# Six of twenty weight loads issued as 120 and 8 rows

## The chip, the core and the metric

The kernel runs on one core of a Trainium2 chip. The metric is the device time of one execution in microseconds (us); less is better. A core has a matrix engine (PE, whose weight loads the profile lists apart as PEld), three engines for elementwise work (DVE, ACT, POOL), a sequencer that here issues every data transfer (SP), and 16 DMA engines that move the bytes.

## What is computed

Block-sparse attention (4 batches, 8 heads, 768 positions, head size 64, blocks of 32), followed by a gated channel mixer over the 512 channels. Cut to what matters:

```python
mask = |blk_i - blk_j| <= 1, or either block is the first or the last, or a sampled block
attn = softmax(where(mask, q @ k.T / sqrt(64), -1e9));  x = attn @ v   # (4, 768, 512)
x_prev = x shifted by one position
xk = mu_k * x + (1 - mu_k) * x_prev;  xr = mu_r * x + (1 - mu_r) * x_prev
k = maximum(xk @ w_k, 0)            # w_k: 512 x 1024
v = (k * k) @ w_v                   # w_v: 1024 x 512
out = sigmoid(xr @ w_r) * v         # w_r: 512 x 512
```

The three weight matrices arrive as 8-byte floats and are turned on the chip into pairs of 4-byte parts.

## The kernel before

**Attention.** The 24 query blocks are worked through in 26 units. Each of the first 22 handles one query block of all four batches and all heads: SP fetches the queries (`q`, L305), the keys (`KA`, L284 and L332) and the values (`VA`, L297 and L349), PE forms scores (`s`, L402), DVE and ACT make the softmax, and PE multiplies by the values (`o`, L436 for the first four units, L475 after). Three of the key blocks and three of the value blocks of a unit are sampled, so SP reads their numbers from `packed` (L266) and computes the address before each transfer. `KA` and `VA` have few slots: the keys of a later unit may be fetched only when PE has read those of an earlier one.

**Weights.** `weight(i, name, src)` (L179) is called twenty times: i = 0 to 3 for the four row blocks of `w_r`, 4 to 11 for the eight blocks of `w_k`, 12 to 19 for the eight row blocks of `w_v`. Each call plans one transfer "w{i} load" (L187) of 128 rows of 4,096 bytes (512 KB) from HBM into the 128 partitions of `raw`, and then six operations on ACT, DVE and POOL that read `raw` and end in the pair of parts `w`: "size" (`wmag`, L201), "tail", "sign", "join", "hi" (L242) and "lo" (L246).

**Mixer.** Twelve tiles of 256 positions: PE computes `r` (L716), `h` (L737) and `v` (L772), which read the weights `w`.

**Order.** Every operation of the kernel stands in one list, and a table of numbers written out by hand (`ORDER`) gives the sequence in which they are emitted. Each engine runs its own in that sequence and waits on semaphores. The twenty weight loads lie in the first 90 us among the fetches of the first units. SP is the only issuer of transfers, and each transfer counts up one of eight semaphores (DMAHW0 to DMAHW7), used in turn; before it is issued SP waits until the transfer that used that semaphore last, eight issues earlier, has landed.

Of the kernel before, what the change touches and what calls it, by code (L numbers as in the profile page):

```python
# [10 lines left out]
I32 = mybir.dt.int32  # L11
# [8 lines left out]
P = 128  # L20
# [75 lines left out]
def block_sparse_attention_channel_mix(  # L96
# [3 lines left out]
    nc = tc.nc  # L100
# [3 lines left out]
    plan = Plan()  # L104
    unit = WIDE_SCALE if wide else 1.0
    PE, ACT, DVE, POOL, SP = "PE", "ACT", "DVE", "POOL", "SP"

    def buf(shape, dtype, tag, bufs, name, pool=sb):
        return Buf(pool, shape, dtype, tag, bufs, name)
# [4 lines left out]
    def choose(name, ways, **more):  # L114

        engine, ns, port, fn = ways[CHOICE.get(name, 0)]
        if "codes" in more:
            more["code"] = more["codes"][CHOICE.get(name, 0)]
        plan.add(name, engine, ns, fn, port=port, ways=[w[:3] for w in ways], **more)
# [59 lines left out]
    def weight(i, name, src):  # L179

        w = buf([P, 2, 512], F32R, f"w{i}", 1, f"w{i}")
        raw = buf([P, 512, 2], I32, f"w{i}", 1, f"raw{i}")
        f = buf([P, 512], F32, "zr", 3, f"wf{i}")
        mag = buf([P, 512], F32, "kk", 3, f"wmag{i}")
        weight_of[name] = w
        words = 2 if wide else 1
        plan.add(f"w{i} load", SP, 480, lambda: nc.sync.dma_start(  # L187
            raw.ap.rearrange("p x b -> p (x b)")[:, 0 : 512 * words], src.bitcast(I32)), writes=[(raw,)], size=262144 * words)

        def high():  # L190
            return raw.ap[:, :, 1] if wide else raw.ap.rearrange("p x b -> p (x b)")[:, 0:512]

        def shorts(which):
            return raw.ap.bitcast(U16)[:, :, which]

        def halves(dtype, which):
            return f.ap.bitcast(dtype).rearrange("p (a b) -> p a b", b=2)[:, :, which]

        def size():
            if wide:  # L200
                nc.scalar.activation(mag.ap, high().bitcast(F32), AF.Copy, scale=2.0**-111)  # L201

        plan.add(f"w{i} size", ACT, 565, size, reads=[(raw,)], writes=[(mag,)])

        def tail():
            if wide:
                nc.vector.tensor_scalar(out=halves(U16, 0), in0=shorts(1), scalar1=13, scalar2=None, op0=ALU.logical_shift_right)

        def tail_pool():
            if wide:  # L210
                nc.gpsimd.tensor_scalar(out=halves(U16, 0), in0=shorts(1), scalar1=2.0**-13, scalar2=2.0**-14 - 0.5, op0=ALU.mult, op1=ALU.add)

        def tail_act():
            if wide:
                nc.scalar.activation(halves(U16, 0), shorts(1), AF.Copy, scale=2.0**-13, bias=2.0**-14 - 0.5)

        choose(f"w{i} tail", [(DVE, 338, 338, tail), (POOL, 900, 0, tail_pool), (ACT, 640, 0, tail_act)], reads=[(raw,)], writes=[(f, 0)])

        def sign():
            if wide:  # L220
                nc.vector.tensor_scalar(out=halves(U16, 1), in0=shorts(3), scalar1=0x8000, scalar2=None, op0=ALU.bitwise_and)

        def sign_act():
            if wide:
                nc.scalar.activation(halves(F16, 1), high().bitcast(F32), AF.Copy, scale=2.0**-60)

        def sign_pool():
            if wide:
                nc.gpsimd.tensor_scalar(out=halves(F16, 1), in0=high().bitcast(F32), scalar1=2.0**-60, scalar2=None, op0=ALU.mult)

        choose(f"w{i} sign", [(DVE, 338, 338, sign), (ACT, 630, 0, sign_act), (POOL, 1650, 0, sign_pool)], reads=[(raw,)], writes=[(f, 1)])

        def join():
            if wide:
                nc.vector.scalar_tensor_tensor(
                    out=f.ap.bitcast(I32), in0=mag.ap.bitcast(I32), scalar=3, in1=f.ap.bitcast(I32),
                    op0=ALU.logical_shift_left, op1=ALU.bitwise_or)
            else:
                nc.vector.tensor_copy(out=f.ap.bitcast(I32), in_=high())

        plan.add(f"w{i} join", DVE, 603, join, reads=[(raw,), (mag,), (f, 0, 1)], writes=[(f,)], port=603)
        choose(f"w{i} hi", [(ACT, 524, 0, lambda: nc.scalar.copy(w.ap[:, 0, :], f.ap)), (POOL, 632, 0, lambda: nc.gpsimd.tensor_copy(w.ap[:, 0, :], f.ap))],  # L242
               reads=[(f,)], writes=[(w, 0)])

        def rest(by):
            by.tensor_tensor(out=w.ap[:, 1, :], in0=f.ap, in1=w.ap[:, 0, :], op=ALU.subtract)  # L246

        choose(f"w{i} lo", [(DVE, 603, 603, lambda: rest(nc.vector)), (POOL, 1262, 0, lambda: rest(nc.gpsimd))], reads=[(f,), (w, 0)], writes=[(w, 1)])

    def weights():  # L250
        jobs = [(("r", c), w_r[c * P : (c + 1) * P, :]) for c in range(CC)]
        jobs += [(("k", c, f), w_k[c * P : (c + 1) * P, f * 512 : (f + 1) * 512]) for f in range(2) for c in range(CC)]
        jobs += [(("v", f), w_v[f * P : (f + 1) * P, :]) for f in range(FC)]
        for i, job in enumerate(jobs):
            weight(i, *job)
# [388 lines left out]
    def split_x(t, which, i0, many, name):  # L644
# [13 lines left out]

        for h in range(CC // MIX):
            f = buf([P, MIX, tw], F32, "mix", 1, f"{name}f{h}")  # L660
            for i in range(MIX):
                c = h * MIX + i
                d = buf([P, tw], F32, "dif", 1, f"{name}d{c}")
# [17 lines left out]
                ], reads=[(d,), (x, *ready), (mk, 2 + which)], writes=[(f, i)])  # L681
            cs = slice(h * MIX, (h + 1) * MIX)

            def rest(by, f=f, cs=cs):
                by.tensor_tensor(out=dst.ap[:, 1, cs], in0=f.ap, in1=dst.ap[:, 0, cs], op=ALU.subtract)

            choose(f"{name} hi {h}", [
                (ACT, 66 + 0.895 * MIX * tw, 0, lambda f=f, cs=cs: nc.scalar.copy(dst.ap[:, 0, cs], f.ap)),
                (POOL, 290 + 0.72 * MIX * tw, 0, lambda f=f, cs=cs: nc.gpsimd.tensor_copy(dst.ap[:, 0, cs], f.ap)),
# [94 lines left out]
    def mixer():  # L784
        xr = xk = None
        for place, t in enumerate(TILES):
# [21 lines left out]
            for i in range(2):  # L808
# [3 lines left out]
             writes=[(mk, 0)], table="exp")  # L812
# [20 lines left out]
X_FROM = 6  # L833
MOVE_FROM = 4

MIX = 2
LAST = 10
TILES = [*range(1, NTILE - 1), 0, NTILE - 1]
# [156 lines left out]
```

## Time and profile before

| | us |
|---|---|
| median of 3 runs | 518.51 |
| lowest, highest | 516.83, 521.39 |
| the profiled execution, its own time | 516.33 |
| span of that execution from the first to the last instruction | 514.6 |
| PE busy in it | 480.9 (93%) |
| PE idle from 40 to 100 us | 7.15 |
| mean busy share of the 16 DMA engines from 40 to 60 us | 0.98 |

In the rows below, times count from the start of the span. "Busy" leaves out sequencer work. A releaser is what ended an engine's wait; "issue" means that the engine waited for nothing that the profile shows. Queue q1 carries the transfers that the program issues, queues q8 and q14 carry instructions.

### The profile page before, as it was taken

Reading aid. Unit: us, or ns where it says so; the run is one execution under the profiler, and the core shown is the slowest. Engines: PE = TensorE matmul, PEld = TensorE weight load, DVE = VectorE, ACT = ScalarE, POOL = GpSimd, SP = SyncE. Lnnn points to the kernel's source line nnn. Section 1 sums busy time; section 2 is a strip of 40 time slices with the busy share of each in tenths; the row PEclk is TensorE's granted clock in tenths of the full one; section 3 lists DMA queues with packets and bytes.
Section 4 is the critical chain, followed back from the end, with each engine's and each line's share of the span. In section 5 each row is a group of like instructions: output and inputs, shape, how many; then the busy total and the mean of one; then the engine's idle time right before and its main releaser. Section 6 shows DMA issues by size and latency. Waiting matters only on the chain.

```text
span 514.6 us, 18098 instructions
## 1 busy us (share of the span) xinstructions
PE 480.9 (93%) x7384; PEld 399.9 (78%) x7384; DVE 320.7 (62%) x608; ACT 306.4 (60%) x701; POOL 207.5 (40%) x253
## 2 busy tenths in 40 slices
PE   4567899999999998999999999999999999999997
PEld 4254577788788787878778878878778879889896
DVE  3667989786786765775675766664765653334231
ACT  2887988867745646546665846655546574455341
POOL 2435546352610723244442432234543525434531
PEclk9689999999999999999999999999999999999999
DMA  7999999798878889888898888999669653100101
GB/s 265 368 343 379 350 337 310 245 279 249 266 214 252 228 217 270 225 258 236 256 264 240 222 258 265 289 275 340 186 158 309 162 137 85 29 22 20 42 22 41
DMA packets 58052, 114.65 MB, mean 223 GB/s; under 512 B 7665, under 2 KB 20721, under 8 KB 55026
## 3 DMA queue, kind: packets, MB, share of 16 engines
q1 hardware_dynamic: 57970, 113.50, 72.3%
q8 instruction: 58, 0.95, 0.7%
q14 instruction: 24, 0.20, 0.1%
HBM read 77.82 MB, written 6.29 MB: 163 GB/s over the span
## 4 chain that ended last, share of the span: by engine, by line
PE 78%; DMA 8%; SPq 4%; ACT 4%; issue 3%; DVE 2%; POOL 1%; POOLq 0%
PE v L772 22%; PE h_2p L737 7%; PE h_0p L737 6%; PE s L402 6%; PE h_1p L737 6%; PE r_1p L716 6%; PE o L475 6%; PE r_0p L716 6%; PE h_3p L737 6%; DMA VA<-vt 3%; DMA KA<-kt 3%; PE sw L496 2%; PE o L538 2%; ACT p L452 1%; SPq L349 1%
## 5 line engine op out<-in xcount | busy, mean ns | idle before, releaser
L772 PE MATMUL v<-w,k 128*128 128x512 f32 (+1 forms) x600 | 138.9, 385 | 0.0
L772 PEld LDWEIGHTS v<-w,k 128*128 128x128 f32 x600 | 107.9, 188 | 26.7 <-issue 4.6
L402 PE MATMUL s<-KA,q 64*32 64x256 f32 x1408 | 47.6, 391 | 15.7 <-DMA raw<-w_k 10.7
L412 DVE TENSOR_REDUCE nm<-s 128x4 f32<-128x1024 f32 x44 | 53.0, 1215 | 14.3 <-PE s L402 14.0
L452 ACT ACTIVATE p<-s,nm 128x256 f32<-128x256 f32 x144 | 60.6, 479 | 0.6
L455 DVE STREAM_TRANSPOSE r<-p 128x1024 f32<-128x1024 f32 x36 | 43.6, 1229 | 10.9 <-ACT p L452 7.1
L402 PEld LDWEIGHTS s<-KA,q 64*32 64x32 f32 x1408 | 26.2, 109 | 30.2 <-POOL w L246 10.7
L475 PEld LDWEIGHTS o<-VA,pt 128*32 128x32 f32 x2304 | 33.9, 109 | 6.6 <-issue 4.4
L716 PE MATMUL r_0p<-w,xr 128*128 128x512 f32 x144 | 36.8, 400 | 1.3 <-issue 1.3
L475 PE MATMUL o<-VA,pt 128*32 128x65 f32 x2304 | 37.3, 221 | 0.8 <-DMA VA<-vt 0.7
L737 PE MATMUL h_2p<-xk,w 128*128 128x256 f32 x288 | 37.8, 284 | 0.2 <-ACT h_0k L752 0.2
L737 PEld LDWEIGHTS h_0p<-xk,w 128*128 128x128 f32 x288 | 35.6, 189 | 3.0 <-issue 1.6
L737 PE MATMUL h_0p<-xk,w 128*128 128x256 f32 x288 | 37.1, 282 | 0.8 <-issue 0.4
L737 PE MATMUL h_3p<-xk,w 128*128 128x256 f32 x288 | 37.4, 285 | 0.0
L737 PEld LDWEIGHTS h_3p<-xk,w 128*128 128x128 f32 x288 | 35.6, 190 | 2.4 <-issue 1.2
L716 PE MATMUL r_1p<-w,xr 128*128 128x512 f32 x144 | 37.2, 398 | 0.0
L737 PEld LDWEIGHTS h_2p<-xk,w 128*128 128x128 f32 x288 | 35.7, 191 | 1.9 <-issue 0.8
L737 PEld LDWEIGHTS h_1p<-xk,w 128*128 128x128 f32 x288 | 35.3, 189 | 2.3 <-DVE rx L576 1.0
L737 PE MATMUL h_1p<-xk,w 128*128 128x256 f32 x288 | 37.0, 283 | 0.0
L666 ACT ACTIVATE xr_0d<-xt,mk 128x128 f32<-128x128 f32 x48 | 19.3, 403 | 21.9 <-DVE xr_0f L673 15.9
L716 PEld LDWEIGHTS r_0p<-w,xr 128*128 128x128 f32 x144 | 26.2, 188 | 7.7 <-issue 1.8
L716 PEld LDWEIGHTS r_1p<-w,xr 128*128 128x128 f32 x144 | 26.0, 189 | 5.3
(237 smaller groups left out, 818.8 us busy)
## 6 DMA issues: line engine op xcount, KB each, us to landing
VA<-vt SPq DMA_DIRECT2D x92, 260.0 KB, 4.3
KA<-kt SPq DMA_DIRECT2D x89, 256.0 KB, 4.2
pt<-r SPq DMA_DIRECT2D x72, 256.0 KB, 4.9
VA<-vw SPq DMA_DIRECT2D x24, 260.0 KB, 5.5
KA<-kq SPq DMA_DIRECT2D x16, 384.0 KB, 5.0
ptw<-rw SPq DMA_DIRECT2D x32, 192.0 KB, 3.8
out<-z SPq DMA_DIRECT2D x23, 256.0 KB, 3.8
q<-qt SPq DMA_DIRECT2D x22, 256.0 KB, 5.8
```

Source lines behind the costliest of these rows:

```text
L349: nc.sync.dma_start(near_values(chunk, j), vt[bass.ds(sampled_block(n, NRAND + j, nc.sync), 1)].rearrange("o w x -> w (o x)"))
L402: nc.tensor.matmul(s.ap[ROWS[j], row, a * 256 : (a + 1) * 256].rearrange("p (n x) -> p n x", x=BLK), q.ap[half, (hp * QB + j) * BLK : (hp ...
L412: nc.vector.tensor_reduce(out=nm.ap.rearrange("p (r a) -> p r a", r=2), in_=s.ap.rearrange("p r (a x) -> p r a x", a=2), axis=AX.X, op=ALU ...
L452: plan.add(f"u{name} exp {i}", ACT, 365, lambda row=row, a=a, i=i: nc.scalar.activation(squares()[:, :, :, i, :], s.ap[:, row, a * 256 : ( ...
L455: plan.add(f"u{name} turn", DVE, N_TURN, lambda: nc.vector.transpose(out=r.ap[:, :, gi].rearrange("p j c i x -> p j (c i x)"), in_=squares ...
L475: nc.tensor.matmul(o[gi].ap[ROWS[j], i * DV : (i + 1) * DV], pt.ap[:, j, gi, g, 2 * row + a, :], VA.ap[:, c0 + g, j, h * DV : (h + 1) * DV ...
L496: nc.tensor.matmul(s.ap[HALF[a], row, 0:W], q.ap[half, 2 * hp * BLK : 2 * (hp + 1) * BLK], wide_keys(b, hp)[half, k * W : (k + 1) * W], st ...
L538: nc.tensor.matmul(o.ap[ROWS[2 * a + e], c * DV : (c + 1) * DV], pt.ap[:, 2 * a + e, row, n, :], VA.ap[:, c1, part, h * DV : (h + 1) * DV] ...
L666: nc.scalar.activation(parts(d.ap), cols(c, 0), AF.Copy, scale=mk.ap[:, which, c : c + 1])
L716: nc.tensor.matmul(pr.ap[:, 0:512], xr.ap[:, a, c, :], weight_of["r", c].ap[:, w, :], start=(c == 0 and m == 0), stop=(c == CC - 1 and m = ...
L737: nc.tensor.matmul(ph.ap[:, ff * TT : (ff + 1) * TT], weight_of["k", c, f2 // 2].ap[:, w, f % 4 * P : (f % 4 + 1) * P], xk.ap[:, a, c, :], ...
L772: nc.tensor.matmul(pv.ap[:, 0:width], k2.ap[:, a, f, i * P : (i + 1) * P], weight_of["v", f].ap[:, w, cs], start=(f == 0 and m == 0), stop ...
```

## The change

For the weights in `CUT` (i = 4, the first block of `w_k`, and 13, 14, 15, 18, 19 of `w_v`) the load is issued as two transfers, the first of rows 0 to 119 and the second of rows 120 to 127, instead of one of 128 rows. Both go to the same buffer `raw`, and the bytes moved are the same. The other fourteen loads and the table `ORDER` are unchanged.

```diff
+        parts = [slice(0, FEWER), slice(FEWER, P)] if i in CUT else [slice(0, P)]
+
+        def fetch():
+            for part in parts:
+                nc.sync.dma_start(raw.ap.rearrange("p x b -> p (x b)")[part, 0 : 512 * words], src[part].bitcast(I32))
-        plan.add(f"w{i} load", SP, 480, lambda: nc.sync.dma_start(
-            raw.ap.rearrange("p x b -> p (x b)")[:, 0 : 512 * words], src.bitcast(I32)), writes=[(raw,)], size=262144 * words)
+        plan.add(f"w{i} load", SP, 480 * len(parts), fetch, writes=[(raw,)], size=262144 * words, dmas=len(parts))
...
+CUT, FEWER = (4, 13, 14, 15, 18, 19), 120
```

On SP, the third of the six cut loads (w14) stands between the last of three sampled key fetches and a key fetch of the unit after. Before (the names are out<-in; what is waited for stands in brackets):

```order
140 L332 DMA KA<-kt 128x512 [waits DMAHW3_49]
141 L187 DMA raw_1121<-w_v 128x1024 [waits DMAHW4_49]
142 L284 DMA KA<-kt 128x512 [waits DMAHW5_49,PE_49]
143 L187 DMA raw_1135<-w_v 128x1024 [waits DMAHW6_49]
144 L305 DMA q_1143<-qt 128x512 [waits DMAHW7_49]
```

And of the change, at the same place:

```order
142 L337 DMA KA<-kt 128x512 [waits DMAHW5_49]
143 L191 DMA raw_1123<-w_v 120x1024 [waits DMAHW6_49]
144 L191 DMA raw_1123<-w_v 8x1024 [waits DMAHW7_49]
145 L289 DMA KA<-kt 128x512 [waits DMAHW0_49,PE_49]
146 L191 DMA raw_1138<-w_v 128x1024 [waits DMAHW1_49]
147 L310 DMA q_1146<-qt 128x512 [waits DMAHW2_49]
```

One transfer more stands there, it takes a semaphore of its own, and every transfer behind it uses the next semaphore of the eight; nothing else moved. Over the program SP has 640 rows where it had 634.

On ACT, the first reader of the first cut load (w13) stands among the softmax of the third unit. Before:

```order
62 L423 ACTIVATE p_1_775<-s_1_628,nm_1_751 128x256 x2
63 L201 ACTIVATE wmag_818<-raw_673 128x512 [waits DMAHW7_49]
64 L614 COPY xt_663<-tx_811 128x4x4x32 [waits PE_49]
```

Of the change:

```order
62 L428 ACTIVATE p_1_776<-s_1_628,nm_1_752 128x256 x2
63 L206 ACTIVATE wmag_820<-raw_673 128x512 [waits DMAHW7_49,DMAHW0_49]
64 L619 COPY xt_663<-tx_813 128x4x4x32 [waits PE_49]
```

It now waits for both transfers, and the order of the operations on ACT, DVE, POOL and PE is as it was.

## Rows read from the trace of the kernel before

**Rows 1.** The page: span, and busy time, share and instructions of PE and others

```profile
span 514.6 us, 18098 instructions
PE 480.9 (93%) x7384; PEld 399.9 (78%) x7384; DVE 320.7 (62%) x608; ACT 306.4 (60%) x701; POOL 207.5 (40%) x253
```

**Rows 2.** Busy time by stretch: length, engines' busy us (instructions), clock, DMA share, GB/s

```profile
core 0: us, PE busy (x) PEld busy (x) DVE busy (x) ACT busy (x) POOL busy (x), PEclk, DMA share, GB/s
...
40.00:60.00 20.00, 15.04 (x421) 10.87 (x424) 16.31 (x37) 16.92 (x46) 10.74 (x13) 1.00 0.98 368
60.00:80.00 20.00, 18.55 (x415) 15.48 (x397) 18.10 (x33) 17.75 (x44) 10.50 (x14) 1.00 0.96 328
80.00:100.00 20.00, 19.26 (x358) 15.21 (x346) 18.17 (x29) 17.48 (x38) 9.89 (x13) 1.00 0.87 294
100.00:514.60 414.60, 406.27 (x5756) 342.10 (x5748) 245.47 (x469) 228.73 (x526) 162.11 (x198) 1.00 0.68 197
```

**Rows 3.** The chain that ended last, 35 to 100 us: start us, us, what

```profile
43.83 2.62 issue
...
60.79 5.76 DMA KA<-kt
...
84.63 0.74 issue
```

**Rows 4.** Timeline of PE: start us, us, instructions [idle before, releaser]

```profile
46.45 0.43 PE L436 MATMUL o<-VA,pt 128*32 128x65 f32 x14 [2.62 <-issue]
...
56.61 0.66 PE L597 MATMUL tx<-ident,x 128*128 128x128 f32 x4 [1.68 <-ACT pt L375]
...
63.16 1.65 PE L716 MATMUL r_0p<-w,xr 128*128 128x512 f32 x6 [0.53 <-issue]
...
66.68 2.67 PE L402 MATMUL s<-KA,q 64*32 64x256 f32 x64 [0.82 <-DMA KA<-kt]
...
85.37 1.53 PE L402 MATMUL s<-KA,q 64*32 64x256 f32 x47 [0.74 <-issue]
```

**Rows 5.** The page, DMA queues: packets, MB, time as share of 16 engines' span

```profile
q8 instruction: 58, 0.95, 0.7%
```

**Rows 6.** DMA queues, 43.8 to 44.9 us, then 60.5 to 61.7 us

```profile
q8 instruction: 1, 0.02, 5.7%
...
q8 instruction: 1, 0.02, 5.1%
```

**Rows 7.** DMA queues, 79.1 to 82.9 us (no q8 there), then 82.9 to 84.0 us

```profile
q1 hardware_dynamic: 376, 1.29, 91.2%
...
q8 instruction: 1, 0.02, 5.4%
```

**Rows 8.** Timeline of SP's DMA issues: start us, us of issuing

```profile
40.81 0.42 SPq L187 DMA_DIRECT2D raw<-w_v  x1
...
59.81 0.42 SPq L187 DMA_DIRECT2D raw<-w_v  x1
60.79 1.33 SPq L284 DMA_DIRECT2D KA<-kt  x1
...
76.28 0.42 SPq L187 DMA_DIRECT2D raw<-w_v  x1
76.80 0.38 SPq L284 DMA_DIRECT2D KA<-kt  x1
```

**Rows 9.** Instructions on tile raw: ns min/median/max, first and last start; time to landing

```profile
L187 SPq DMA_DIRECT2D raw<-w_k x8: 339/430/576, 1.9 to 47.5; - x8
L187 SPq DMA_DIRECT2D raw<-w_v x8: 417/502/637, 40.8 to 85.6; - x8
...
DMA to landing us min/median/max: 4.0/5.9/9.1
```

**Rows 10.** DMA issues of the whole span: count, KB each, median us to landing

```profile
VA<-vt SPq DMA_DIRECT2D x92, 260.0 KB, 4.3
KA<-kt SPq DMA_DIRECT2D x89, 256.0 KB, 4.2
...
mk<-mu_r SPq DMA_DIRECT2D x1, 2.0 KB, 1.6
```

## The prediction, made before the changed kernel ran

> **What bounds the kernel now.** I read the page first: PE is busy for 480.9 of 514.6 us [rows 1], so only the time in which PE stands still can be won. The table by stretches says where that is. From 100 us to the end PE is busy for 406.27 of 414.60 us, and all six cut loads have been issued before 86 us [rows 2, 9]. From 40 to 100 us PE stands still for 4.96 + 1.45 + 0.74 = 7.15 us, and there the 16 DMA engines are 0.98, 0.96 and 0.87 busy [rows 2]. That stretch is the field of this change, and 7.15 us, 1.4% of the time, is its ceiling.
>
> Next I read what ended PE's waits there. In the chain, and on PE's own timeline, there are two kinds that a transfer can have caused. One is a transfer proper: keys issued at 60.79 us take 5.76 us to land, and PE is idle for 0.82 us before it can start the scores at 66.68 [rows 3, 4]. The other is called "issue": PE idle for 2.62 us before 46.45, 0.53 before 63.16 and 0.74 before 85.37, each in the middle of a run of equal matmuls or with nothing to wait for by the program [rows 3, 4]. The DMA queues tell what these are. Queue q8 moves 58 packets in 0.95 MB, 16 KB each [rows 5]; PE with its weight loads has 14,768 instructions [rows 1], 255 to a packet. So q8 brings PE's instructions in pages. In the stretch 43.8 to 44.9 us, just as PE stops, one such page is moved, and so it is in 60.5 to 61.7 and in 82.9 to 84.0, each shortly before PE goes on [rows 6, 7]. A page takes 5.7% of 16 engines for 1.1 us, or 0.057 x 16 x 1.1 = 1.0 us of one engine. PE goes on at 46.45, 63.16 and 85.37: 1.5 to 1.6 us after the end of the page where one can place it (43.8 + 1.0). So PE waits for a late page, and the page is late because data is in front of it.
>
> [...]
>
> **The change, part by part.** It moves the same bytes. It adds six transfers of 8 rows, six issues on SP, and a second semaphore for the first readers of six buffers. What can help is that rows change their DMA engine. Which engine moves which row the trace does not show. Equal shares would give each of 16 engines 8 of 128 rows; I take it that 120 rows are 8 rows each for 15 engines and nothing for one, and that the last 8 rows go one each to engines that already have eight. The price of a row comes from 40 to 60 us: 368 GB/s over 16 x 0.98 busy engines is 23.5 GB/s for one, so 4,096 bytes cost 0.174 us and 8 rows 1.39 us. A cut load thus frees one engine for 1.39 us and costs some others 0.17 us. If the freed engine is the one that also carries the pages of q8, its queue is the longest, since each page adds 1.0 us to it, and everything that lands on all engines lands when it does.
>
> Term by term, for the case that the freed engine is that one:
>
> - Keys at 60.79 us. The cut load w14 was issued at 59.81, directly in front [rows 8], and a page passed between [rows 6]. The freed engine is 1.39 us ahead, more than the 0.82 us that PE waited. Gain 0.82.
> - Page before 85.37 us. The cut load w18 was issued at 76.28 [rows 8]; with the median landing of 5.9 us [rows 9] its data moves at about 81 to 82 us, in front of the page that starts at about 82.9, with 91.2% of all engines' time on data just before [rows 7]. Freed 1.39, waited 0.74. Gain 0.74.
> - Page before 46.45. The first cut load was issued at 40.81 [rows 8] and lands at about 46.7 by the median, so its data moves behind the page of 43.8. Gain 0.
> - Page before 63.16. The last load of w_k was issued at 47.5 [rows 9] and has landed by 56.6 even at the longest 9.1 us; w14 is behind. Gain 0. The 1.68 us before 56.61 end with ACT [rows 4]. Gain 0.
> - The extra rows on other engines: 0.17 us at each of the two places. Cost 0.35.
> - SP: six issues of 0.50 us (median of w_v, [rows 9]), 3.0 us in all. At 59.81 there is room: the issue ends at 60.23 and the keys go out at 60.79, when PE has freed their slot. At 76.28 there is 0.10 us of room, so the transfers behind go out 0.4 us later. The cover is the queue in the DMA engines: 4.2 us from issue to landing for keys against 1.6 us for the smallest transfer [rows 10]. I take 0; without the cover it is 0.4 us for each load, 2.4 in all. Behind the waiting SP stand keys and values of the next unit, for which PE's scores wait.
> - The second semaphore: the 8 rows land with or a little after the 120, 0 to 0.17 us, and the readers wait far longer in their own engines' queues. Taken as 0.
>
> Sum: -0.82 - 0.74 + 0.35 = -1.2 us. The profiled execution's own time was 516.33, which gives 515.1. The median of the three runs, 518.51, is 2.18 above it, so the forecast for a median is 517.3.
>
> **The rivals.**
>
> *Nothing is won.* The pages of q8 may ride on an engine that the 120 rows still use; then both waits stay. For it: no row names an engine. Against it: nothing either, except that the waits exist. The two extra rows (0.35 us) and up to 2.4 us of SP stay as cost: 516.7 to 519.1 for the profiled execution, 518.9 to 521.3 for the median, most likely at the lower end. [...]
>
> *The whole field is won.* If the freed engine's delay is what holds back all transfers from 41 us on, the waits on SP shrink too, and PE's idle time goes but for the 1.68 us that ACT ends: 7.15 - 1.68 = 5.5 us, a median of 513.0. Against it: the largest piece, 2.62 us, lies in front of the first cut load's data.
>
> *Slower.* A transfer of 120 rows may be spread over fewer engines. Over eight it would be 15 rows for each, and with the extra row 16 instead of 8: 1.39 us more for each cut load. The keys at 60.79 stand behind the third cut load and in part behind the two before, and the page at 82.9 and the last units behind the others; if four to six of them count, that is 5.6 to 8.3 us, a median of 524.1 to 526.8. For it: all transfers of the kernel with many rows have 32 or 128 of them, so none shows what another number does. Against it: 260 KB in 32 rows land in 4.3 us and 256 KB in 128 rows in 4.2 [rows 10], so the number of rows alone has no price. It decides from about 0.9 us per cut load on, which makes 5.2 us over six.
>
> [...]
>
> **How the numbers follow.** The forecast (0.3 to 2.2 us won) has 0.45, nothing won 0.38, the whole field 0.07, slower by spreading 0.10. The first two lie between 516 and 521.3; three runs of the same kernel differ by 4.6 us, so the range goes from 513.5 to 521.5 and leaves out 0.17. About 1%, 5.2 us, is what a measurement of this kernel can tell from no change. Faster by more (below 513.3): the whole field and a little of the forecast, 0.08. Slower by more (above 523.7): most of the spreading, 0.07. Within 1%: 0.85.
>
> **What the profile of the changed kernel would show.** If the forecast holds, PE's idle time before the scores at about 66 us falls from 0.82 to under 0.2, that before 85 us from 0.74 to under 0.2, and the q8 packet of 82.9 comes up to 1.4 us earlier, while 2.62 us before 46.45 stay. If nothing is won, all three rows stay within 0.2 us. If the 120 rows are spread over fewer engines, the median landing of raw rises from 5.9 us to above 7 and the GB/s of 40 to 80 us fall. The prediction is wrong if the page before 46.45 comes earlier (then the freed engine matters beyond its own load's data) or if PE's idle time after 100 us changes by more than 1 us.

## The result: 1.3% slower, and the profile after

The changed kernel takes 524.19 us (median of 16 runs, 519.0 to 527.14) against 517.47 for the kernel before (16 runs on the same chip). The ratio is 1.0127 with a 95% interval of 1.0101 to 1.0154: 6.6 us more, 5.2 to 8.0. The forecast was 517.3, with a range up to 521.5. The profiled execution of the changed kernel took 527.08 us, about 3 more than the median, so its rows are read for where time goes and the sizes come from the ratios.

The page of the changed kernel, span and busy time, and its line on DMA packets:

```profile
span 525.3 us, 18108 instructions
PE 484.6 (92%) x7384; PEld 403.1 (77%) x7384; DVE 319.6 (61%) x608; ACT 306.4 (58%) x701; POOL 206.2 (39%) x253
...
DMA packets 58094, 114.65 MB, mean 218 GB/s; under 512 B 7707, under 2 KB 20763, under 8 KB 55068
```

The same line of the kernel before:

```profile
DMA packets 58052, 114.65 MB, mean 223 GB/s; under 512 B 7665, under 2 KB 20721, under 8 KB 55026
```

The bytes are the same. There are 42 more packets, all under 512 B. If a transfer ends with one short packet on each engine that it uses, that is 6 x (15 + 8 - 16) = 42: the 120 rows ride on 15 engines and the 8 rows on 8, as the prediction assumed. So nothing was spread over fewer engines. PE is busy 3.7 us longer and stands still 7.0 us longer (525.3 - 484.6 = 40.7 against 33.7).

Busy time by stretch, after (length, then busy us of each engine with its instructions, clock, DMA share, GB/s), which answers [rows 2]:

```profile
40.00:60.00 20.00, 13.93 (x362) 10.82 (x361) 13.31 (x31) 13.06 (x36) 9.00 (x11) 0.83 1.03 298
60.00:80.00 20.00, 16.14 (x306) 11.70 (x307) 14.54 (x24) 15.13 (x37) 8.82 (x12) 0.91 0.99 274
80.00:100.00 20.00, 17.28 (x290) 14.61 (x288) 17.11 (x35) 15.07 (x36) 8.53 (x10) 1.00 1.02 288
100.00:525.30 425.30, 415.95 (x5958) 350.03 (x5958) 251.96 (x479) 236.80 (x543) 164.89 (x202) 1.00 0.68 198
```

From 40 to 100 us PE stands still for 6.07 + 3.86 + 2.72 = 12.65 us against 7.15. The two columns at the right say why: the DMA engines are as busy as before or busier (1.03, 0.99, 1.02; a share a little over 1, up to 1.04 in the loads alone below, stands for full), and yet they move 298 and 274 GB/s where they moved 368 and 328, and from 80 to 100 us they need a share of 1.02 for 288 GB/s where 0.87 was enough for 294. The engines work as long or longer and bring less. After 100 us PE's idle time is 9.35 us against 8.33, which is 1.02 more.

PE's timeline, after, in the order of [rows 4] (start, us, instructions, [idle before, releaser]):

```profile
45.04 0.43 PE L441 MATMUL o<-VA,pt 128*32 128x65 f32 x14 [1.48 <-issue]
54.65 3.70 PE L441 MATMUL o<-VA,pt 128*32 128x65 f32 x128 [3.90 <-DMA VA<-vt]
67.24 1.65 PE L721 MATMUL r_0p<-w,xr 128*128 128x512 f32 x6 [1.22 <-issue]
72.58 3.61 PE L407 MATMUL s<-KA,q 64*32 64x256 f32 x64 [2.64 <-issue]
92.15 1.02 PE L407 MATMUL s<-KA,q 64*32 64x256 f32 x18 [1.43 <-issue]
93.64 1.52 PE L407 MATMUL s<-KA,q 64*32 64x256 f32 x46 [0.47 <-issue]
```

SP's timeline, after (start, us of issuing; x2 on `raw` are the two transfers of a cut load):

```profile
41.06 0.82 SPq L191 DMA_DIRECT2D raw<-w_v  x2
45.50 0.50 SPq L302 DMA_DIRECT2D VA<-vt  x1
63.52 0.82 SPq L191 DMA_DIRECT2D raw<-w_v  x2
64.44 0.36 SPq L289 DMA_DIRECT2D KA<-kt  x1
82.59 0.82 SPq L191 DMA_DIRECT2D raw<-w_v  x2
83.51 0.36 SPq L289 DMA_DIRECT2D KA<-kt  x1
```

The chain that ended last, after, in order of time (start, us, what), as [rows 3]:

```profile
45.50 9.10 DMA VA<-vt
...
63.14 6.24 DMA KA<-kt
69.39 8.80 DMA VA<-vt
...
82.59 8.98 DMA raw<-w_v
```

The largest wait is new: PE stands still for 3.90 us until values land that were issued at 45.50, behind the cut load of 41.06, and took 9.10 us; values took 4.3 in the median before [rows 10]. This wait alone is not the loss: PE's idle time from 40 to 60 us grew by only 1.1 us (6.07 against 4.96), and a kernel with whole loads that is not slower has nearly the same wait (below, at the clock). The page wait before 46.45 became shorter, 1.48 us instead of 2.62, and its page was moved from about 42.3 us instead of 43.8.

Of the two waits that the forecast wanted to remove, the first has grown: the scores after `r_0p` wait 2.64 us (0.82 before). At the second place there are now two waits. The one in the middle of the scores, which was 0.74 us before 85.37, is 0.47 us before 93.64; an instruction page that was moved from about 91.3 us fits it. In front of the same scores a new wait of 1.43 us has come. The view calls all three "issue", but at 72.58 and 92.15 no instruction page was late. Between 68 and 72 us the queues (packets, MB, share) show no q8:

```profile
DMA packets 367, 1.00 MB, mean 249 GB/s; under 512 B 45, under 2 KB 45, under 8 KB 365
## 3 DMA queue, kind: packets, MB, share of 16 engines
q1 hardware_dynamic: 367, 1.00, 102.2%
```

The next page was moved from about 72.4 us, too late to have let PE go on at 72.58, since its packet alone takes 1.1 us of one engine (6.8% of 16 engines from 72 to 73 us); and from 88 to 91.2 us there is none either. What the scores at 72.58 and 92.15 read are keys issued right behind a cut load, at 64.44 and at 83.51. At the landing times of this stretch (6.24 to 9.10 us in the chain) they land at 70.7 to 73.5 and at 89.8 to 92.6, which fits PE's starts at 72.58 and 92.15. That it was these keys is argued from the order and the times, not shown. The instructions on `raw`, after, end with the landing times of its loads; the median is 7.1 us where it was 5.9 [rows 9]:

```profile
DMA to landing us min/median/max: 6.0/7.1/8.5
```

### The profile page after: what moved, and what is told of

Read it like the earlier page. It is cut to its first block, busy times and chain, and to the rows that moved or that the text cites. A ratio compares the mean times of both kernels' runs of the same rounds, so it can differ in the third digit from the quotient of the medians.

```text
span 525.3 us, 18108 instructions
## 1 busy us (share of the span) xinstructions
PE 484.6 (92%) x7384; PEld 403.1 (77%) x7384; DVE 319.6 (61%) x608; ACT 306.4 (58%) x701; POOL 206.2 (39%) x253
## 4 chain that ended last, share of the span: by engine, by line
PE 66%; DMA 17%; SPq 9%; issue 3%; DVE 3%; ACT 2%; ACTq 0%; DVEq 0%
PE v L777 17%; PE h_1p L742 6%; PE r_0p L721 6%; PE h_0p L742 6%; DMA VA<-vt 5%; PE s L407 5%; PE h_2p L742 5%; PE h_3p L742 5%; PE r_1p L721 5%; PE o L480 4%; DMA KA<-kt 4%; SPq L468 3%; PE o L543 2%; PE sw L501 2%; DMA q<-qt 2%
## 5 line engine op out<-in xcount | busy, mean ns | idle before, releaser
L407 PE MATMUL s<-KA,q 64*32 64x256 f32 x1408 | 49.1, 402 | 20.1 <-DMA raw<-w_k 10.7
L407 PEld LDWEIGHTS s<-KA,q 64*32 64x32 f32 x1408 | 27.5, 111 | 34.7 <-issue 13.4
L572 DVE TENSOR_TENSOR x<-o,R 128x128 f32<-128x128 f32 x96 | 25.2, 322 | 8.4 <-ACT xt L594 3.9
```

The lines of the kernel that those rows point to most:

```text
L407: nc.tensor.matmul(s.ap[ROWS[j], row, a * 256 : (a + 1) * 256].rearrange("p (n x) -> p n x", x=BLK), q.ap[half, (hp * QB + j) * BLK : (hp ...
L572: nc.vector.tensor_tensor(out=to[:, :, 2 * e : 2 * e + 2], in0=o[i].ap.rearrange("p (c e v) -> p c e v", e=2, v=DV)[:, :, e, 0:D].rearrang ...
```

## The experiments

After the result three theories stood. **A**: the rows of a 120-row transfer are dealt to the engines so that their packets take longer, and a load costs more DMA time though the bytes are the same; that several engines then work in the same part of the on-chip memory at once was the author's guess at the reason. **B**: fewer engines work on it. **C**: the second transfer costs, by its issue on SP, its semaphore or its completion.

One measure is used throughout. In a stretch in which only such loads move, a row of 4,096 bytes costs 16 engines x share x 4,096 B / GB/s of engine time. A whole load of 128 rows, spread over 16 engines (share 1.00 to 1.01 alone, below), is 8 such rows for each.

**The loads alone.**

```python
for i in range(NL):                                        # one group: eight loads
    nc.sync.dma_start(bufs[i][0:120, :], rows(i)[0:120])
    nc.sync.dma_start(bufs[i][120:128, :], rows(i)[120:128])
wait()                                                     # then the next group
```

> This kernel computes nothing of the reference (its output is zeros): it only loads blocks of w_v, in stretches of eight buffers each, with a wait for all of them between stretches: 128 rows (line 31), 120 rows (34), 120 and 8 rows (37, 38), 8 rows (41), 112 rows (44), 112 and 16 (47, 48), 64 rows (51), 64 and 64 (54, 55), 96 rows (58), 120 and 128 rows in turn (61, 62), 128 rows again (65). Theory A, rows on the wrong engines (a transfer of fewer than 128 rows deals its rows to the DMA engines so that several of them write to the same part of the on-chip memory at once): the packets of 120, 112, 64 and 96 rows are longer than those of 128 rows, whose packet takes about 0.16 to 0.17 us; I expect 0.25 us or more, so 250 to 300 GB/s where 128 rows reach about 400. Theory B, fewer engines (15 of 16 for 120 rows, 8 for 8): packets stay at 0.16 to 0.17 us, 120 rows reach 15/16 of the rate of 128, and 112 and 64 rows the same rate as 128. Theory C, issue and semaphores: neither packet times nor rates differ by more than 5%; 8 rows alone take about 2 us each to land.

Busy time by stretch of that kernel (length, DVE, POOL, clock, DMA share, GB/s). In this order: 128 rows, 120 rows, 120 and 8, 112 and 16, 64 rows, 64 and 64:

```profile
27.00:33.00 6.00, 0.00 (x0) 0.00 (x0) 1.00 0.76 309
40.00:50.00 10.00, 0.00 (x0) 0.00 (x0) 1.00 0.97 227
60.00:72.00 12.00, 0.00 (x0) 0.00 (x0) 1.00 0.97 225
...
106.00:116.00 10.00, 0.00 (x0) 0.00 (x0) 1.00 1.03 263
124.00:130.00 6.00, 0.00 (x0) 0.00 (x0) 1.00 1.04 212
138.00:150.00 12.00, 0.00 (x0) 0.00 (x0) 1.00 1.04 231
```

(The first stretch includes the end of its group, hence 0.76.) A row costs 16 x 0.76 x 4,096 / 309,000 = 0.161 us in a load of 128 rows, 0.280 in one of 120, 0.282 with the 8 rows, 0.257 in 112 and 16, 0.321 in 64, 0.295 in 64 and 64. A load cut into 120 and 8 rows costs 8 x (0.282 - 0.161) = 0.97 us more of all engines, six of them 5.8 us. B falls: 112 and 16 rows are both multiples of 16, use all engines (share 1.03), and cost nearly as much.

**Other cuts in the kernel**, into 112 and 16 rows and into two halves:

```diff
-CUT, FEWER = (4, 13, 14, 15, 18, 19), 120
+CUT, FEWER = (4, 13, 14, 15, 18, 19), 112    # and 64
```

> The changed kernel with the six loads cut as 112 and 16 rows, both of which divide by 16. Theory A: as slow as 120 and 8 rows, ratio 1.008 to 1.018 to the kernel before, and GB/s of 40 to 80 us near 290 instead of 350. Theory B (fewer engines): all 16 engines have equal shares again, ratio 0.998 to 1.003. Theory C (a second issue and semaphore for each of six loads): as slow as the change, ratio 1.008 to 1.018, but with packets as short as before.

> The changed kernel with the six loads cut as 64 and 64 rows. Theory A: slower than before, 1.008 to 1.02, since both halves are dealt unlike 128 rows. Theory B: 0.998 to 1.003. Theory C: 1.008 to 1.018, packets as short as before.

Measured: 1.0106 (1.0053 to 1.0160) and 1.0118 (1.0076 to 1.0160), both about the loss of the change, though by the rows no engine has more or fewer than in a whole load. The GB/s from 40 to 80 us, expected near 290 for 112 and 16 rows, were 335 and 312 there, less of a fall than expected; for the two halves they were 310 and 274.

**The loads whole, and 8 rows more.** The six loads are issued whole; behind each, its last 8 rows are transferred once more, to a spare place in HBM.

```diff
+            nc.sync.dma_start(raw.ap.rearrange("p x b -> p (x b)")[:, 0 : 512 * words], src.bitcast(I32))
+            if i in CUT:
+                nc.sync.dma_start(spare[i], src[FEWER:P].bitcast(I32))
```

> The kernel before with a further transfer behind each of the six loads, of 8 rows of 4096 bytes to a scratch array in HBM that nothing reads: the loads stay whole, and the extra issue, the extra semaphore and a transfer of 8 rows on the same DMA engines stay. Theory A and theory B: 0.998 to 1.004. Theory C: 1.008 to 1.018, as slow as the change.

Measured: 1.0017 (0.9987 to 1.0048). The six issues and six semaphores more cost nothing that can be measured, even with 0.2 MB more moved. C falls for the issue. Nothing reads the spare rows, so a reader's wait for a second transfer is not tested here; the next kernel and the even and odd halves below have it.

**Cut by columns**, twice 128 rows of 2,048 bytes:

```diff
-        parts = [slice(0, FEWER), slice(FEWER, P)] if i in CUT else [slice(0, P)]
+        parts = [slice(0, 512), slice(512, 1024)] if i in CUT else [slice(0, 1024)]
...
+                nc.sync.dma_start(raw.ap.rearrange("p x b -> p (x b)")[:, part], src.bitcast(I32)[:, part])
```

> The six loads of the change are again issued as two transfers each, but cut by columns: twice 128 rows of 2,048 bytes instead of 120 and 8 rows of 4,096. Both transfers keep 128 rows. Theory A (the price is a longer packet, which a transfer has when its row count is not 128): no such packets here, so the time is that of the kernel before, ratio 0.998 to 1.004, and the windows 60 to 80 and 80 to 100 us show about the GB/s of before (328, 294). Rival (a second transfer into the same buffer costs by itself, by its issue, its semaphore or its smaller pieces): about as slow as the change, 1.008 to 1.015.

Measured: 1.0044 (1.0002 to 1.0085), just above the first expectation and below the second. Twice as many packets may cost a little, 2.3 us by the middle of the interval; by it most of the change's loss is not there.

**Half of the cut loads.**

```diff
-CUT, FEWER = (4, 13, 14, 15, 18, 19), 120
+CUT, FEWER = (4, 13, 14), 120                # and (15, 18, 19)
```

> Only the first half of the cut is left: loads 4, 13 and 14 as 120 and 8 rows, loads 15, 18 and 19 whole. Theory A (each cut load takes 1.2 us more of all DMA engines, and nearly all of it reaches the end because the engines are full from 40 to 100 us): 3 x 1.2 = 3.6 us at most, about half of the change's loss, ratio 1.004 to 1.008. Rival (one place decides: the keys fetched right behind load 14 at 59.8 us): the whole loss, 1.010 to 1.015. Rival (the loss lies with the last three): 0.998 to 1.003.

> Only the second half of the cut is left: loads 15, 18 and 19 as 120 and 8 rows, loads 4, 13 and 14 whole. Theory A: the other half of the loss, ratio 1.004 to 1.008, and the two halves together make the 1.0127 of the change. Rival (one place among the first three decides): 0.998 to 1.003. Rival (the last three decide): 1.010 to 1.015.

Measured: 1.0063 (1.0018 to 1.0108) and 1.0026 (0.9986 to 1.0066). The first fits its half; the middle of the second lies below its range, though its interval reaches into it. Together they make 1.0089. The intervals are wide: the second alone would also fit "nothing", and the first reaches into the range of "all". This pair does not decide between six equal shares and a heavier first half.

**All twenty.**

```diff
+CUT, FEWER = tuple(range(20)), 120
```

> All twenty weight loads are issued as 120 and 8 rows. Theory A (1.2 us of full DMA engines more for each cut load, as measured by the loads alone): up to 20 x 1.2 = 24 us; where the first loads of the program find PE without work anyway all of it counts, so 15 to 24 us slower, ratio 1.03 to 1.047. Rival (the loss is a matter of where these six stand, not of each cut load): not above 1.02.

Measured: 1.0477 (1.0392 to 1.0561), 24.7 us, or 1.24 us for each cut load, just above the top of the expectation. (These expectations reckoned with 1.2 us for each cut load; the row prices above give 0.97.) It is the cut load that costs, not where these six stand.

**Which rows, alone.** The cause could still lie on the side of HBM, or in the row count as such. So eight loads at a time again, in other choices of rows, always the same bytes of HBM for 64 rows:

```python
nc.sync.dma_start(bufs[i][0:128:2, :], rows(i)[0:64])      # the even partitions
nc.sync.dma_start(bufs[i][0:64, :], rows(i)[0:64])         # 64 in a row
```

> The kernel computes nothing: eight loads of the weights at a time, alone on the chip, in rows of 4,096 bytes, each group in another choice of rows; then whole and 120-row copies from HBM to HBM. Measured is the time of a packet, from the share and the count of packets in a stretch inside each group. 128 rows should give 0.16 us a packet and 120 rows 0.28 us again. Theory A (several engines work in the same part of the on-chip memory at once; which part a row lies in goes by its partition): rows 8 to 127 as long as rows 0 to 119, since the count decides how rows are dealt; 64 even partitions (0, 2, ... 126) another length than 64 in a row (0.32 us), since they lie elsewhere; from HBM to HBM 120 rows no longer per packet than 128. Rival D (the price is paid on the side of HBM, by rows read in another order): 64 even partitions as long as 64 in a row, since the same rows of HBM are read, and from HBM to HBM 120 rows 1.5 times and more as long per packet as 128. By the engine count that divides the rows, 124 rows ride on 4 engines, a share of about 0.25.

By stretch (columns as above): 128 rows; rows 0 to 119; rows 8 to 127; 64 even; 64 in a row; 32 in a row; 16 in a row; 124 rows:

```profile
22.00:30.00 8.00, 0.00 (x0) 0.00 (x0) 1.00 1.01 402
36.00:46.00 10.00, 0.00 (x0) 0.00 (x0) 1.00 0.97 226
56.00:66.00 10.00, 0.00 (x0) 0.00 (x0) 1.00 0.96 241
76.00:82.00 6.00, 0.00 (x0) 0.00 (x0) 1.00 0.74 259
86.00:94.00 8.00, 0.00 (x0) 0.00 (x0) 1.00 1.04 207
99.00:103.00 4.00, 0.00 (x0) 0.00 (x0) 1.00 0.82 166
106.00:110.00 4.00, 0.00 (x0) 0.00 (x0) 1.00 0.43 98
114.00:142.00 28.00, 0.00 (x0) 0.00 (x0) 1.00 0.26 104
```

A row costs 0.165, 0.281, 0.261, 0.187, 0.329, 0.324, 0.288 and 0.164 us. The pair in the middle decides: the same 64 rows of HBM, the same count, the same size cost 0.187 us each in the even partitions and 0.329 in partitions 0 to 63. (The stretch of the even ones includes the end of its group, hence 0.74.) So it is the place in the on-chip memory, not HBM and not the count. Full engines are not needed for the price: 16 rows in a row leave engines idle (share 0.43 over the stretch shown, the end of their group included) and still cost 0.288. (The 0.82 of the 32 rows comes from the end of their group.) The 124 rows ride on 4 engines (share 0.26 of 16) and cost 0.164, no more than rows of whole loads. That fits the guess (few engines are at work, and few can meet) and does not show it. The copies from HBM to HBM told nothing, since they moved in packets of another size (1.41 MB in 44 long packets, 32 KB each).

**The same cut, even and odd.** In the kernel, the 64 even and the 64 odd rows instead of two halves; and, to keep the 15 engines of the change, 60 even, 60 odd and 8 rows:

```diff
-        parts = [slice(0, FEWER), slice(FEWER, P)] if i in CUT else [slice(0, P)]
+        parts = [slice(0, P, 2), slice(1, P, 2)] if i in CUT else [slice(0, P)]
```

```diff
+        parts = [slice(0, FEWER, 2), slice(1, FEWER, 2), slice(FEWER, P)] if i in CUT else [slice(0, P)]
```

> The six loads are cut in two halves again, but by turns: the 64 even rows and the 64 odd rows instead of rows 0 to 63 and 64 to 127. Row count, bytes, issues and semaphores are those of the cut into two halves, which cost 1.0118. Theory A (what costs is where in the on-chip memory the rows of one transfer lie; alone, 64 even rows took 0.15 us a packet and 64 rows in a row 0.26): the time of the kernel before, ratio 0.997 to 1.005. Rival (a transfer that has fewer than 128 rows costs, whichever rows they are): 1.008 to 1.016.

> The six loads as three transfers: even rows 0 to 118, odd rows 1 to 119, rows 120 to 127. The rows are shared out as in the change (60 rows are a multiple of 15, so one engine of 16 has none of the 120), but those of a transfer lie two apart. Theory A: most of the loss of the change is gone, ratio 0.997 to 1.006. On the premise of the forecast (the engine left out is the one that carries the instruction pages) it would be up to 1.2 us faster than the kernel before, 0.997 to 0.999, and the wait of PE near 66 us and that near 85 us would fall under 0.2 us; without that premise both stay. Rival (a transfer of other than 128 rows costs, whichever rows): 1.010 to 1.020.

> The kernel computes nothing: eight loads at a time alone on the chip, cut in several ways; measured is the time of a packet in a stretch inside each group. By theory A: 128 rows 0.15 us a packet (completions included), 64 even and 64 odd rows the same, 60 even and 60 odd rows 0.15 to 0.20, every fourth row 0.15; rows 0 to 119 about 0.25 and two halves in a row about 0.26, as measured before. By the rival (the row count alone) all groups but the whole ones are at 0.23 or more.

Alone, by stretch: 128 rows; 64 even and 64 odd; 60 and 60; 60, 60 and 8; rows 0 to 119; two halves; every fourth row, four times:

```profile
21.00:30.00 9.00, 0.00 (x0) 0.00 (x0) 1.00 1.00 390
35.50:45.00 9.50, 0.00 (x0) 0.00 (x0) 1.00 0.94 319
52.00:64.00 12.00, 0.00 (x0) 0.00 (x0) 1.00 0.88 263
71.00:86.00 15.00, 0.00 (x0) 0.00 (x0) 1.00 0.77 231
92.00:105.00 13.00, 0.00 (x0) 0.00 (x0) 1.00 0.96 236
112.00:126.00 14.00, 0.00 (x0) 0.00 (x0) 1.00 1.04 234
134.00:151.00 17.00, 0.00 (x0) 0.00 (x0) 1.00 0.68 205
```

A row costs 0.168, 0.193, 0.219, 0.218, 0.267, 0.291 and 0.217 us. Even and odd rows come near whole loads; 60 and 60 and every fourth row lie between. In the groups of rows taken by turns SP issues without a pause, at 0.59 us for a transfer of 64 or 32 rows and 0.79 us for one of 60, and the engines are not full (0.94 to 0.68); with full engines, as in the kernel, these rows may cost more. The expectation counted packets, with the short ones at a transfer's end: so counted (16 x share x length / packets, of which there are 931, 952 and 1,275) the three are 0.15, 0.18 and 0.15 us, as expected, but a load pays by its rows.

In the kernel the even and odd halves measure 1.0007 (0.9963 to 1.0050), where the halves in a row cost 1.0118: same count of transfers, rows, bytes and semaphores. Its readers wait for two transfers, too. Its busy time by stretch shows GB/s near those of before (368, 328, 294) [rows 2]; the halves in a row have 310, 274 and 291:

```profile
40.00:60.00 20.00, 14.96 (x414) 10.50 (x420) 17.28 (x37) 17.29 (x45) 12.29 (x15) 1.00 0.96 348
60.00:80.00 20.00, 17.79 (x358) 14.70 (x345) 16.82 (x30) 16.71 (x41) 7.72 (x12) 1.00 0.98 329
80.00:100.00 20.00, 20.00 (x419) 16.11 (x408) 18.53 (x32) 17.82 (x40) 10.48 (x13) 1.00 0.90 294
```

60, 60 and 8 rows measure 1.0085 (1.0049 to 1.0122), a miss of the expectation "most of the loss is gone", and by the middle below the rival's range, too. One thing that differs from the even and odd halves is the time on SP: the three transfers of the third cut load take it 2.83 us to issue, and 0.81 + 0.80 + 0.46 = 2.07 us alone, where two halves take twice 0.59 alone and the two transfers of the change 0.82:

```profile
61.98 2.83 SPq L191 DMA_DIRECT2D raw<-w_v  x3
```

Whether this, or the price of rows that were measured with engines not full, makes the miss was not tested.

**Does the row price carry the time?** For each kernel: the price of a row alone, less that of a whole load in the same run, times 8 rows, times the number of cut loads; beside it what was measured.

| cut | row alone, us (whole) | loads | worked out, us | measured, us (95%) |
|---|---|---|---|---|
| 120 and 8 (the change) | 0.282 (0.161) | 6 | 5.8 | 6.6 (5.2 to 8.0) |
| 112 and 16 | 0.257 (0.161) | 6 | 4.6 | 5.5 (2.7 to 8.3) |
| 64 and 64 in a row | 0.295 (0.161) | 6 | 6.4 | 6.1 (3.9 to 8.3) |
| 60, 60 by twos, and 8 | 0.218 (0.168) | 6 | 2.4 | 4.4 (2.5 to 6.3) |
| 64 and 64 by twos | 0.193 (0.168) | 6 | 1.2 | 0.4 (-1.9 to 2.6) |
| 120 and 8, first three | 0.282 (0.161) | 3 | 2.9 | 3.3 (0.9 to 5.6) |
| 120 and 8, last three | 0.282 (0.161) | 3 | 2.9 | 1.3 (-0.7 to 3.4) |
| 120 and 8, all | 0.282 (0.161) | 20 | 19.4 | 24.7 (20.3 to 29.0) |

Six of eight lie inside the interval, but the intervals are 3 to 9 us wide, so the table supports the size and no more. The cut into 60, 60 and 8 is worked out 0.1 us below its interval and "all" 0.9 us below: there something is added that the row price doesn't hold. For the first SP's longer issue is a candidate; the runs don't decide it. That nearly all of the added engine time arrives at the end is argued: the DMA engines are full from 40 to 100 us while PE waits for what they bring.

**What the clock has to do with it.** The granted clock of the changed kernel is 0.83 from 40 to 60 us and 0.91 from 60 to 80, where it was 1.00; from 53 to 58 us and from 73 to 76 us it was 0.50, the first from within PE's wait of 3.90 us before 54.65 on, the second after its wait of 2.64 before 72.58. That is not what makes the loss by itself: the kernel with whole loads and 8 rows more has 0.83 in the same 20 us, and PE busy for 484.8 us like the changed kernel's 484.6, and is not slower (1.0017). It also has a wait of 3.40 us for values at the place of the changed kernel's 3.90, so neither belongs to the cut alone. How much of the changed kernel's loss passes through the lower clock, once PE waits, the runs don't tell. The stretch of 40 to 60 us with whole loads and 8 rows more, and PE's row with that wait:

```profile
40.00:60.00 20.00, 15.22 (x374) 12.01 (x380) 15.23 (x35) 14.95 (x41) 9.37 (x10) 0.83 0.94 331
```

```profile
52.89 3.69 PE L442 MATMUL o<-VA,pt 128*32 128x65 f32 x128 [3.40 <-DMA VA<-vt]
```

## Why the prediction was wrong

**What bounds the kernel: right.** The loss arose in the field that was named, 40 to 100 us: PE's idle time grew by 5.5 us there and by 1.02 after.

**15 engines and 8 engines: right.** The 42 added packets say so, and so do the loads of 60, 60 and 8 rows alone: 251 short packets for 847 rows, 38 to a load of 128 rows, which is 15 + 15 + 8.

**The price of a row: the step that failed.** "4,096 bytes cost 0.174 us and 8 rows 1.39 us" was worked out from a stretch in which all loads were whole, and carried over to rows of a 120-row transfer. There a row costs 0.282 us, and the engines that keep their 8 rows need 2.26 us for them. What was to be won, one engine's 1.39 us, was thus paid for by 0.97 us of all engines, per load, where the sum had 0.17 us of some engines. The terms of the sum (-0.82, -0.74, +0.35) did not come: at the first place PE waited 2.64 us instead of 0.82, at the second 1.43 and 0.47 instead of 0.74.

**Two of its own signs of being wrong came.** The page before 46.45 came earlier, and PE's idle time after 100 us changed by 1.02 us, just over the 1 us that was named. The first was to mean that the freed engine matters beyond its own load's data. The runs don't bear that out: with even and odd halves no engine is freed, and the wait there is 1.03 us. What moves it from kernel to kernel is open.

**"The number of rows alone has no price": a comparison that hid the cause.** 260 KB in 32 rows land as fast as 256 KB in 128 (4.3 and 4.2 us [rows 10]), but those 32 rows are every fourth partition over all 128, as the kernel's own line says:

```python
return VA.ap[slot : P : QB, c].rearrange("p b x -> p (b x)")      # QB = 4
```

They lie apart, like the even rows above. 32 rows in a row cost 0.324 us each. The sentence was true of the number and silent on the place.

**The slower rival: size right, mechanism wrong.** It gave 524.1 to 526.8, and 524.19 was measured, but by fewer engines with 16 rows each. Its signs came true for another reason: the median landing rose to 7.1 us and GB/s fell. So the hit is luck. The signs could not tell the two apart; the count of short packets could (42), and it spoke against fewer engines. With 0.10 the rival had too little chance, since the row that spoke against it was the one of 32 rows.

**SP and the second semaphore at nothing: right**, the issue by the whole loads with 8 rows more (1.0017), the readers' wait for two transfers by the even and odd halves (1.0007).

**The freed engine as the engine of the pages: not settled.** The dearer rows hide it. (The 1.5 to 1.6 us from a page's end to PE's start are 1.5 to 1.7 by the prediction's own figures, which changes nothing.) With 60, 60 and 8 rows, which ride on 15, 15 and 8 engines by the short packets (38 to a load), of the two waits that were to fall below 0.2 us the first is 3.15 us, and the one before 85 us is gone: the 64 scores at 89.27 run without a pause. But it is gone with the even and odd halves too (the 64 scores at 84.63), which ride on 16 engines (191 short packets for 740 rows alone, 16 to 17 for each 64), so this says nothing of a freed engine; and rows are dearer with 60, 60 and 8 (0.218 us alone against 0.193). PE's timeline of that kernel:

```profile
45.62 0.43 PE L441 MATMUL o<-VA,pt 128*32 128x65 f32 x14 [2.06 <-issue]
...
64.39 1.66 PE L721 MATMUL r_0p<-w,xr 128*128 128x512 f32 x6 [0.94 <-issue]
...
70.25 3.67 PE L407 MATMUL s<-KA,q 64*32 64x256 f32 x64 [3.15 <-issue]
...
89.27 1.96 PE L407 MATMUL s<-KA,q 64*32 64x256 f32 x64
```

Also open is the mechanism below theory A. That the price goes by which partitions the rows of one transfer occupy (the same 64 rows: 0.187 and 0.329 us), and that it is absent in the 124 rows on 4 engines (0.164), is shown; why, no run shows.

## What to carry to other kernels

A DMA engine's time for a row belongs to the transfer from which it was measured (alone 0.161 us in whole loads, 0.282 in loads of 120 and 8 rows): before rows are moved from one engine to another, measure the new shape alone, by share and GB/s of a stretch in which nothing else moves. When rows of a 128-partition load have to be split, split them into even and odd halves and not in blocks (here 1.0007 against 1.0118), and best not at all while the DMA engines are the full resource: 60, 60 and 8 rows by turns still cost 1.0085. And when two transfers serve as evidence that a number has no price, look at everything else in which they differ, here the step between their partitions.

## What the runs showed of the hardware

- Rows of 4,096 bytes from HBM cost 0.161 to 0.168 us of a DMA engine in a transfer to all 128 partitions, 0.26 to 0.28 us to 96 to 120 partitions in a row (96: share 1.03 at 256 GB/s, 0.264), 0.29 to 0.33 us to 64 or 32 in a row, and 0.288 to 16 in a row. To 64 even partitions they cost 0.187, to 64 even and 64 odd ones by turns 0.193.
- Whole loads, one behind the other, move at 390 to 402 GB/s, loads of rows 0 to 119 at 226 to 236, of rows 8 to 127 at 241.
- A load of 124 rows rides on 4 engines (share 0.26 of 16) and moves at 104 GB/s.
- A wait that a view calls "issue" is not always a late instruction page: in the 2.64 us before 72.58 no such page was moved until about 72.4.
